# Moving x^T from TensorE to crossbar DMAs in an attention + gated-FFN kernel, with a later FFN and a re-planned order

## The chip, the cores and the metric

One core of one Trainium2 chip. The metric is the device time of one execution in microseconds (us), lower is better. Before: 307.08 us, median of 3 runs (306.74 to 307.47).

The names in what follows: PE is TensorE (matmuls and transposes), ACT is ScalarE, DVE is VectorE, and the sync engine (SP) issues DMAs. PSUM is the memory into which this kernel's matmuls and PE transposes write. A crossbar DMA is one that transposes what it moves (`dma_start_transpose`). It lands when its data is there. The granted clock is the share of its full speed at which PE was clocked.

## The reference, cut to what matters

Block-sparse attention over 4 batches, 8 heads, 768 positions and head size 64, followed by a gated FFN. The mask is 0 or 1 per block of 32 positions.

```python
scores = where(mask, q @ k.T / 8, -1e9)          # per batch and head, 768 x 768
attn = softmax(scores) @ v                       # -> x: (3072 tokens, 512)
gate = 1 / (1 + exp(-(x @ w_gate)))              # 512 -> 1536
out  = (gate * (x @ w_val)) @ w_out              # 1536 -> 512, float32
```

## The kernel before

The tokens are cut into 12 units of 256. A unit has four pairs of heads. For each pair the kernel makes the transposed scores (PE), exponentials (ACT), mask products (DVE), value products (PE), and the division by the row sum (DVE), which gives x16, tokens on partitions. The gate and value products of the FFN need x with features on partitions: x^T. The kernel before makes it with two PE transposes per pair and a copy out of PSUM by DVE or ACT:

```python
def turn(self, eng):
    for s in range(2):
        nc.tensor.transpose(
            m16(self.bank2.slot)[:, s * 128 : (s + 1) * 128], self.x16[:, s, :, :], ident)

def evac(self, eng):
    ...                                                   # allocates xT of the unit once
    copy(eng, xTs[self.n][0][:, self.p, :], m16(self.bank2.slot)[:, 0:UQ])

def xt(self):
    c = plan.add([(PE, 0.12)], self.turn, [self.normed], take=[self.bank2])
    ...
    plan.add([(DVE, 0.29), (ACT, 0.37)], self.evac, [c] + deps, free=[self.bank2])
```

All work is first entered as tasks in a `Plan`. The plan simulates a greedy schedule with rough costs, and then emits the instructions in the order that came out. Its costs never reach the chip; they only decide the order on each engine. At run time an engine takes its instructions in that order and waits on semaphores.

A unit's pass has six slots. A slot has two score steps, and one FFN part of an earlier unit to keep PE busy beside the exponentials:

```python
for sl in range(6):
    scores(flat[2 * sl : 2 * sl + 2])
    if sl >= 2:
        for i in range(3):
            ffn[n - 1].f(3 * (sl - 2) + i)       # gate and value products: 8 matmuls each
            if i == 0 and sl % 3 != 1:
                do(valued, do_value)             # value products of a pair
    elif n > 1:
        ffn[n - 2].y(sl)                         # output product: 12 matmuls
    ...
```

The softmax here doesn't subtract the row's maximum and nothing guards it: scores larger than these inputs give would overflow.

## Time and profile before

| | before |
|---|---|
| median | 307.08 us |
| span of the profiled run | 304.5 us |
| PE busy | 291.4 us |
| DVE / ACT busy | 200.9 / 210.7 us |
| one unit, in the steady part | 23.09 us |

First come the span, the busy times and the busy shares in 40 slices of the page of the kernel before (9 is 90% or more).

```profile
span 304.5 us, 7858 instructions
...
PE 291.4 (96%) x3326; PEld 209.6 (69%) x3326; DVE 200.9 (66%) x474; ACT 210.7 (69%) x340; POOL 48.5 (16%) x65
...
PE   3978999999999999999999999999999999999994
...
ACT  3669986776776776776776776776776776774431
PEclk9999999999999999999999999999999999999998
```

PE is full from the fifth slice (about 30 us) to the last but one. ACT is full only around the fourth and fifth slice.

A busy PE is not yet a PE with no time to give, since matmul ends are modelled. So the chain that ended last was read, in order of time, for one unit of the kernel before. Columns: start us, duration us, what. L571 is the output product, L466 the x transposes, L406 scores, L445 value products, L532 gate and value products.

```profile
94.91 2.59 PE m L571 x12
97.50 0.11 PE m L466 x2
97.61 0.54 PE s L406 x8
98.16 2.70 PE m L571 x12
100.85 0.11 PE m L466 x2
100.97 0.54 PE s L406 x8
...
109.05 0.11 PE m L466 x2
109.16 0.54 PE s L406 x8
...
118.01 2.59 PE m L571 x12
```

Each piece starts where the last one ended: PE's instruction stream alone sets the pace, 118.01 - 94.91 = 23.1 us per unit. A pair of transposes advances the chain by 0.11 us. The same transposes look far dearer in the table of groups of the kernel before (columns: busy us, mean ns of one, idle time ahead):

```profile
L466 PE MATMUL m<-ident,x 128*128 128x128 f16 x96 | 13.3, 221 | 0.1
L227 DVE COPY xT<-m 128x256 f16<-128x256 f16 x31 | 9.0, 292 | 10.9 <-PE m L466 10.9
L225 ACT COPY xT<-m 128x256 f16<-128x256 f16 x17 | 6.3, 371 | 0.0
```

221 ns is the time of one transpose through the pipeline. The next matmul starts long before that is over.

Last, the DMAs of the sync queue in the kernel before, with median us from issue to landing:

```profile
out_dram<-ysb SPq DMA_DIRECT2D x24, 256.0 KB, 2.0
kT<-kp SPq DMA_TRANSPOSE x3, 7.2
qT<-qp SPq DMA_TRANSPOSE x3, 7.1
```

The transposes of k and q, three of each and 768 KB apiece, are the only crossbar DMAs of this kernel.

### The profile page before, as it was taken

The page shows a single profiled execution, that of the slowest core. Times are in us where ns is not written, and L with a number is a line of the kernel's source. Part 1 is how long each engine was busy: PE and PEld are TensorE (multiplying, and loading weights), DVE is VectorE, ACT ScalarE, POOL GpSimd, SP SyncE. Part 2 cuts the span into 40 slices and gives each one's busy share as a digit, 9 for nine tenths or more (in the row PEclk, how much of TensorE's full clock was granted, in tenths as well). Part 3 has the DMA queues.
Part 4 walks back from the last instruction along what each step waited for, and adds up shares of the span by engine and source line. Part 5 has one row for each costly group of instructions (what it writes and reads, how often), then busy time and mean ns, then how long its engine had stood idle before and what let it go on. Part 6 is the DMA issues. An engine that isn't in the chain of part 4 may idle for free.

```text
span 304.5 us, 7858 instructions
## 1 busy us (share of the span) xinstructions
PE 291.4 (96%) x3326; PEld 209.6 (69%) x3326; DVE 200.9 (66%) x474; ACT 210.7 (69%) x340; POOL 48.5 (16%) x65
## 2 busy tenths in 40 slices
PE   3978999999999999999999999999999999999994
PEld 1355785786786786786686686687687687687771
DVE  4669878876676678676676577576576577576240
ACT  3669986776776776776776776776776776774431
POOL 8943000494000059200000000000000000000000
PEclk9999999999999999999999999999999999999998
DMA  7999999999500699930100580100100100100101
GB/s 100 181 203 202 206 204 183 223 160 131 128 1 2 158 154 124 154 74 2 71 2 0 113 168 1 71 2 2 69 2 2 69 2 4 69 2 2 69 2 70
DMA packets 62768, 25.75 MB, mean 85 GB/s; under 512 B 45812, under 2 KB 59660, under 8 KB 62732
## 3 DMA queue, kind: packets, MB, share of 16 engines
q0 software_dynamic: 40400, 14.16, 40.8%
q1 hardware_dynamic: 22332, 11.09, 15.0%
q8 instruction: 26, 0.43, 0.6%
q14 instruction: 10, 0.08, 0.1%
HBM read 28.39 MB, written 6.29 MB: 114 GB/s over the span
## 4 chain that ended last, share of the span: by engine, by line
PE 93%; ACT 2%; DMA 1%; DVE 1%; issue 1%; POOL 1%; POOLq 0%
PE m L532 42%; PE m L571 21%; PE s L406 13%; PE m L445 13%; PE m L466 2%; DMA v<-in_v_dram 1%; ACT pt L416 1%; PE m L303 1%; PE m L338 1%; ACT mask L225 1%; DVE pt L422 0%; DVE kT L227 0%; POOL k L178 0%; POOL q L178 0%; ACT ysb L582 0%
## 5 line engine op out<-in xcount | busy, mean ns | idle before, releaser
L416 ACT ACTIVATE pt<-s 128x1024 f16<-128x1024 f32 x144 | 140.1, 1026 | 4.6 <-PE s L406 3.7
L422 DVE TENSOR_TENSOR pt<-pt,mask 128x1024 f16<-128x1024 f16 x144 | 97.2, 687 | 38.8 <-ACT pt L416 38.4
L532 PE MATMUL m<-xT,wg 128*128 128x256 f16 x576 | 86.7, 273 | 0.0
L532 PE MATMUL m<-xT,wv 128*128 128x256 f16 x576 | 86.4, 273 | 0.0
L543 ACT ACTIVATE th<-m 128x256 f32<-128x256 f32 x144 | 54.6, 390 | 43.8 <-PE m L532 36.0
L548 DVE SCALAR_TENSOR_TENSOR ht<-th,m 128x256 f16<-128x256 f32 x144 | 57.3, 418 | 16.4 <-ACT th L543 14.8
L571 PE MATMUL m<-wo,ht 128*128 128x512 f16 x288 | 66.0, 379 | 0.0
L532 PEld LDWEIGHTS <-wv 128*128 128x128 f16 x576 | 56.3, 98 | 6.5
L532 PEld LDWEIGHTS <-wg 128*128 128x128 f16 x576 | 51.3, 97 | 12.5 <-issue 7.2
L445 PE MATMUL m<-vex,pt 128*128 128x65 f16 x1152 | 46.5, 196 | 1.8 <-ACT mask L225 1.6
L445 PEld LDWEIGHTS <-pt 128*128 128x128 f16 x1152 | 42.6, 99 | 7.6 <-issue 5.3
L571 PEld LDWEIGHTS <-ht 128*128 128x128 f16 x288 | 26.6, 98 | 30.7 <-issue 2.1
L406 PE MATMUL s<-qT,kT 64*128 64x256 f16 x576 | 47.1, 279 | 0.6 <-DVE qT L227 0.3
L582 ACT ACTIVATE ysb<-m 128x512 f32<-128x512 f32 x24 | 14.3, 597 | 35.3 <-PE m L571 35.3
L406 PEld LDWEIGHTS <-kT 64*128 64x128 f16 x576 | 22.0, 95 | 15.8 <-issue 8.6
L622 POOL DMA_DIRECT2D kp<-in_k_dram x16 | 13.0, 822 | 64.1 <-DMA kT<-kp 37.9
L455 DVE RECIPROCAL rz<-m 128x4 f32<-128x4 f32 x48 | 8.7, 182 | 19.5 <-PE m L445 18.8
L457 DVE TENSOR_TENSOR x<-m,rz 128x256 f16<-128x256 f32 x48 | 20.4, 425 | 1.7
L227 DVE COPY xT<-m 128x256 f16<-128x256 f16 x31 | 9.0, 292 | 10.9 <-PE m L466 10.9
L466 PE MATMUL m<-ident,x 128*128 128x128 f16 x96 | 13.3, 221 | 0.1
L622 POOL DMA_DIRECT2D qp<-in_q_dram x16 | 13.1, 827 | 0.7 <-DVE pt L422 0.4
L466 PEld LDWEIGHTS <-x 128*128 128x128 f16 x96 | 9.0, 98 | 6.1 <-DVE x L457 0.7
(36 smaller groups left out, 71.9 us busy)
## 6 DMA issues: line engine op xcount, KB each, us to landing
out_dram<-ysb SPq DMA_DIRECT2D x24, 256.0 KB, 2.0
v<-in_v_dram POOLq DMA_DIRECT2D x3, 768.0 KB, 10.9
wg<-in_moe_w_gate_dram POOLq DMA_DIRECT2D x4, 384.0 KB, 12.7
wv<-in_moe_w_val_dram POOLq DMA_DIRECT2D x4, 384.0 KB, 13.6
wo<-in_moe_w_out_dram POOLq DMA_DIRECT2D x3, 512.0 KB, 16.7
kp<-in_k_dram POOLq DMA_DIRECT2D x16, 96.0 KB, 5.1
qp<-in_q_dram POOLq DMA_DIRECT2D x16, 96.0 KB, 4.5
k<-in_k_dram POOLq DMA_DIRECT2D x4, 192.0 KB, 5.6
```

Of the source, the lines that this page charges most:

```text
L406: nc.tensor.matmul(score[self.bank.slot][:, a, i, :], kT[b % 2][o : o + D, p, t * 128 : (t + 1) * 128], qT[b % 2][o : o + D, p, u * UQ : ( ...
L416: nc.scalar.activation(self.pt, score[self.bank.slot], AF.Exp, bias=0.0, scale=SCALE)
L422: nc.vector.tensor_tensor(self.pt, self.pt, m.unsqueeze(1).broadcast_to([128, 2, 2, UQ]), op=ALU.mult,)
L445: nc.tensor.matmul(self.acc[:, s, a, :], self.steps[t // 2].pt[:, a, t % 2, s * 128 : (s + 1) * 128], vex[self.b % 2][:, 2 * self.p + a, t ...
L457: nc.vector.tensor_tensor(self.x16, self.acc[:, :, :, 0:D], rz.broadcast_to([128, 2, 2, D]), op=ALU.mult,)
L466: nc.tensor.transpose(m16(self.bank2.slot)[:, s * 128 : (s + 1) * 128], self.x16[:, s, :, :], ident,)
L532: nc.tensor.matmul(pg[:, i, :], w[:, c, f * 128 : (f + 1) * 128], xTs[self.n][0][:, c, :], start=(c == 0), stop=(c == 3),)
L543: nc.scalar.activation(th, spare[bank.slot][:, 0:UQ], AF.Tanh, bias=0.0, scale=0.5)
L548: nc.vector.scalar_tensor_tensor(self.ht[:, f, :], in0=box[0], scalar=1.0, in1=spare[bank.slot][:, UQ : 2 * UQ], op0=ALU.add, op1=ALU.mult,)
L571: nc.tensor.matmul(spare[bank.slot], self.ht[:, f, s * 128 : (s + 1) * 128], wo[:, f, :], start=(f == 0), stop=(f == NF - 1),)
L582: nc.scalar.activation(ysb, spare[bank.slot], AF.Copy, bias=0.0, scale=0.5)
L622: nc.gpsimd.dma_start(dst[:, p, :, a, :], src[b, 2 * p + a].rearrange("(n t) d -> n t d", t=NT),)
```

## The change

From unit 2 on, x^T of a pair comes from one crossbar DMA of 64 KB in place of two PE transposes and a copy. Such a DMA takes longer than the PE path. So the FFN parts come one slot later, and the plan counts a latency of 6 us for it. The output product is planned in three parts of four matmuls. The ring of x16 grows from 4 to 6 buffers.

```diff
+FFN_LAG = 3
+        def xbar(self, eng):
+            ...
+            nc.sync.dma_start_transpose(
+                xTs[self.n][0][:, self.p, :].rearrange("a (s n) -> a s n", s=2),
+                self.x16.rearrange("a s h d -> a (s h d)"),
+            )
         def xt(self):
+            if self.n >= 2:
+                deps = [used["xT"][self.n - XB]] if self.n >= XB else []
+                c = plan.add([(DMA, 0.05)], self.xbar, [self.normed] + deps, lag=6.0)
+                used["x16"].append(c)
+                xdone[self.n].append(c)
+                return
 ...
-            a = plan.add([(PE, 2.6)], mm, self.gated, at=land["wo", 2], take=[bank])
+            a = None
+            for f0 in range(0, NF, 4):
+                a = plan.add([(PE, 0.88)], y_mm(f0, f0 + 4),
+                    self.gated[f0 : f0 + 4] + ([] if a is None else [a]), ...)
 ...
-            if sl >= 2:
-                for i in range(3):
-                    ffn[n - 1].f(3 * (sl - 2) + i)
-                    ...
-            elif n > 1:
-                ffn[n - 2].y(sl)
+            part = parts.popleft() if n > 1 or sl >= FFN_LAG else []
+            for i, fn in enumerate(part):
+                fn()
+                if i == 0 and sl % 3 != 1:
+                    do(valued, do_value)
```

More of the change, by code (lines that the diff above doesn't have):

```diff
@@ L455, in norm @@
             nc.vector.reciprocal(rz, self.acc[:, :, :, D : D + 1])
-            self.x16 = work.tile([128, 2, 2, D], f16, tag="x16", bufs=4, name="x16")
+            self.x16 = work.tile([128, 2, 2, D], f16, tag="x16", bufs=6, name="x16")
             nc.vector.tensor_tensor(
@@ L483, in value @@
             read["pv", self.b, self.p] = [a]
-            self.normed = plan.add([(DVE, 0.6)], self.norm, [a] + ring("x16", 4),
+            self.normed = plan.add([(DVE, 0.6)], self.norm, [a] + ring("x16", 6),
                                    free=[self.bank])
-        def xt(self):
+        def xbar(self, eng):
+            if not xTs[self.n]:
+                xTs[self.n].append(
+                    work.tile([128, NP, UQ], f16, tag="xT", bufs=XB, name="xT")
+                )
+            nc.sync.dma_start_transpose(
+                xTs[self.n][0][:, self.p, :].rearrange("a (s n) -> a s n", s=2),
+                self.x16.rearrange("a s h d -> a (s h d)"),
+            )
+        def xt(self):
+            if self.n >= 2:
[4 more added lines that the diff above has]
+                return
             c = plan.add([(PE, 0.12)], self.turn, [self.normed], take=[self.bank2])
@@ L567, in y, with y_mm, go @@
             bank = Bank("m")
-            def mm(eng):
-                for f in range(NF):
-                    nc.tensor.matmul(
-                        spare[bank.slot],
-                        self.ht[:, f, s * 128 : (s + 1) * 128],
-                        wo[:, f, :],
-                        start=(f == 0),
-                        stop=(f == NF - 1),
-                    )
+            def y_mm(f0, f1):
+                def go(eng):
+                    for f in range(f0, f1):
+                        nc.tensor.matmul(
+                            spare[bank.slot],
+                            self.ht[:, f, s * 128 : (s + 1) * 128],
+                            wo[:, f, :],
+                            start=(f == 0),
+                            stop=(f == NF - 1),
+                        )
+                return go
             def evac(eng):
@@ L594, in evac @@
                 )
-            a = plan.add([(PE, 2.6)], mm, self.gated, at=land["wo", 2], take=[bank])
+            a = None
+            for f0 in range(0, NF, 4):
+                a = plan.add(
+                    [(PE, 0.88)],
+                    y_mm(f0, f0 + 4),
+                    self.gated[f0 : f0 + 4] + ([] if a is None else [a]),
+                    at=land["wo", f0 // 4],
+                    take=[bank] if f0 == 0 else [],
+                    lag=0.0 if f0 < 8 else None,
+                )
             if s == 1:
@@ L704 @@
     later(1)
+    parts = deque()
+    for F in ffn:
+        for i in range(4):
+            parts.append([lambda F=F, f=f: F.f(f) for f in range(3 * i, 3 * i + 3)])
+        parts.extend([[lambda F=F, s=s: F.y(s)] for s in range(2)])
     for n in range(1, len(units)):
@@ L718 @@
                 scores(run)
-            if sl >= 2:
-                for i in range(3):
-                    ffn[n - 1].f(3 * (sl - 2) + i)
-                    if i == 0 and sl % 3 != 1:
-                        do(valued, do_value)
-            elif n > 1:
-                ffn[n - 2].y(sl)
-            if sl == 0:
+            part = parts.popleft() if n > 1 or sl >= FFN_LAG else []
[3 more added lines that the diff above has]
+                    do(valued, do_value)
+            if not part and sl % 3 != 1:
                 do(valued, do_value)
@@ L736 @@
     do(valued, do_value)
-    ffn[-2].y(0)
-    do(turned, Pair.xt)
-    ffn[-2].y(1)
-    for f in range(NF):
-        ffn[-1].f(f)
-    ffn[-1].y(0)
-    ffn[-1].y(1)
+    for part in parts:
+        for fn in part:
+            fn()
+        do(turned, Pair.xt)
     plan.run()
```

## The prediction

> **What bounds the kernel.** TensorE. The page's first part has PE busy 291.4 of 304.5 us (96%); the stretch table shows 12.00 of 12.00 us from 36 us on. The chain of waits that ended last is 93% PE: gate/value products 42%, output product 21%, scores 13%, values 13%, x transposes 2%. ACT (210.7 us) and DVE (200.9 us) have slack. Idle PE time lies before 36 us and in the last 4 us. From unit 2 on a unit takes 23.1 us (output products start at 71.82, 94.91, 118.01 us in the chain).
>
> **Removed.** 80 of the 96 x transposes on PE, and 40 of the 48 evacuations to x^T (DVE 292 ns, ACT 371 ns each); the instruction lists agree. A transpose's duration is 221 ns, but it is pipelined: in the chain a pair takes 0.11 us, and the score group after it 0.54 us with or without a pair ahead. So 40 x 0.11 = 4.4 us of PE time, all on the critical path. The Trainium skill ("TensorE: Matmul & The Clock Gate", Part 4: PE-mode transpose) gives about 275 ns for one in a kernel; charging that would promise about 20 us, which this trace contradicts. The evacuations (about 12 us of DVE and ACT) are off the path, worth nothing directly.
>
> **Added.** 40 crossbar DMAs of 64 KB on the sync queue. The 768 KB ones of k and q (24 blocks of 128x128) take 3.5 to 6.2 us to issue and 7.2 us to land. Scaled to two blocks, I estimate 0.3 to 0.5 us of issue and 2.5 to 3.5 us to landing (the output DMA lands in 2.0). All stay on the one sync stream, as the Trainium skill ("DMA: Bandwidth & Descriptors", Silent corruption) requires.
>
> **Moved.** FFN parts come one slot (3.8 us) later. In the new order, between a unit's last value product and its first gate product stand 16 gate/value matmuls, three score groups, two output products and a value product: 1.75 + 3 x 0.54 + 2 x 2.70 + 0.77 = 9.5 us. Less 0.7 us of normalisation, 8 to 9 us hide a DMA of 3 us, even one slowed by the loads between 57 and 135 us. In the tail 7.8 us of products stand there. The big k/q transposes are queued after a unit's last small one and delay none that is urgent.
>
> Splitting the output product changes no PE work; it matters to the planner alone. Switches after a score group cost 0.11 us; they stay six per unit. Unit period: 23.09 - 0.44 = 22.65 us.
>
> In unit 1, the shift takes gate work away where ACT is full (11.87 of 12 us between 24 and 36 us); I allow 0 to 1.5 us of new idle PE time.
>
> **Prediction.** 307.08 - 4.4 + 0.6 = 303.3 us, range 301.8 to 306.2. Faster by over 2%: 0.04; within 2%: 0.90; slower by over 2%: 0.06.
>
> **Right if** the unit period is 22.65 us; 16 PE transposes are left; small crossbar DMAs land in 2.5 to 4 us, with no PE wait on them; DVE is near 190 us, ACT near 206 us; the first output product starts within 1.5 us of 48.8 us. **Wrong if** PE waits for x^T, the unit period stays at 23.1 us, or PE idles between 28 and 50 us.
>
> **What would make it wrong.** A small crossbar DMA taking over 8 us (fixed cost, the ordered sync queue blocked by an output DMA's wait, or contention with loads): some us in each of ten units, hence slower. Or neighbours' weight loads running better without the transposes: 1 to 2 us more gained.

## The result, and the profile after

| | before | after |
|---|---|---|
| median (4 runs each) | 306.91 us | 301.74 us (301.47 to 302.64) |
| span of the profiled run | 304.5 us | 299.7 us |
| PE busy | 291.4 us | 287.0 us |
| DVE / ACT busy | 200.9 / 210.7 us | 194.4 / 207.4 us |
| one unit, in the steady part | 23.09 us | 22.65 us |

The ratio after to before is 0.9836 (95% interval 0.9808 to 0.9863), hence faster by some 1.6%, within the band of 2%.

The page of the kernel after:

```profile
span 299.7 us, 7758 instructions
...
PE 287.0 (96%) x3246; PEld 203.1 (68%) x3246; DVE 194.4 (65%) x447; ACT 207.4 (69%) x327; POOL 48.5 (16%) x65
```

The chain of the kernel after for one unit. L589 is now the output product, L407 scores, L446 value products, L549 gate and value products:

```profile
94.96 2.69 PE m L589 x12
97.66 0.54 PE s L407 x8
98.20 2.70 PE m L589 x12
100.90 0.77 PE m L446 x24
101.67 0.54 PE s L407 x8
102.21 0.98 PE m L549 x8
...
117.61 1.40 PE m L589 x6
```

The pieces still follow one another without a gap, only the transposes are gone. The unit takes 117.61 - 94.96 = 22.65 us.

The transposes that are left, in the groups of the kernel after, and the crossbar DMAs among its DMA issues:

```profile
L467 PE MATMUL m<-ident,x 128*128 128x128 f16 x16 | 2.4, 231 | 0.1
```

```profile
xT<-x SPq DMA_TRANSPOSE x40, 2.4
```

The new DMAs land after 2.3 us at least, 2.4 in the median and 8.3 at most, among those of the 40 for which the trace has a landing. The last pair's DMA issued at 138.7 us, beside the loads of a later batch, took 5.1 us; the one issued at 161.3 us, with no loads, 2.3 us.

How much latency the order can hide is read from the timeline of the kernel after, around the last pair of a unit:

```profile
92.93 0.43 DVE L458 TENSOR_TENSOR x<-m,rz 128x256 f16<-128x256 f32 x1
93.38 1.17 SPq L493 DMA_TRANSPOSE xT<-x  x1
...
102.14 0.61 PE L549 MATMUL m<-xT,wg 128*128 128x256 f16 x4
```

The division ends at 93.36 us, the DMA is issued at once, and the first gate product that needs it starts 8.76 us later. With 2.4 us to landing, 6.4 us are spare. The 1.17 us in the second line is only the sync engine's issue. The Trainium skill ("Perfetto Trace Analysis", DMA Instruction — HWDGE) says that the profiler's window of such an instruction leaves out the data movement; this trace agrees, 1.17 us against 2.4 us to landing.

One measure is free of the jitter of the start: from the first gate product of the kernel to the end of the last output matmul. In the kernel before it goes from 31.37 to 300.08 us, 268.71 us; after, from 30.99 to 295.78 us, 264.79 us. This stretch is 3.92 us shorter. It is used below as "the stretch".

### The profile page after: what moved, and what is told of

Same layout as the page of the kernel before. It is cut to its first block, busy times and chain, and to the rows that moved or that the text cites. A ratio compares the mean times of both kernels' runs of the same rounds, so it can differ in the third digit from the quotient of the medians.

```text
span 299.7 us, 7758 instructions
## 1 busy us (share of the span) xinstructions
PE 287.0 (96%) x3246; PEld 203.1 (68%) x3246; DVE 194.4 (65%) x447; ACT 207.4 (69%) x327; POOL 48.5 (16%) x65
## 4 chain that ended last, share of the span: by engine, by line
PE 92%; ACT 2%; DMA 2%; DVE 2%; issue 1%; POOL 1%; POOLq 0%
PE m L549 43%; PE m L589 21%; PE s L407 13%; PE m L446 12%; DMA v<-in_v_dram 2%; ACT pt L417 1%; PE m L304 1%; PE m L339 1%; ACT mask L226 1%; DVE pt L423 0%; DVE kp L365 0%; POOL k L179 0%; PE m L467 0%; POOL q L179 0%; ACT xT L226 0%
## 5 line engine op out<-in xcount | busy, mean ns | idle before, releaser
L423 DVE TENSOR_TENSOR pt<-pt,mask 128x1024 f16<-128x1024 f16 x144 | 98.9, 689 | 50.2 <-ACT pt L417 49.8
L549 PE MATMUL m<-xT,wg 128*128 128x256 f16 x576 | 86.8, 273 | 0.0
L549 PE MATMUL m<-xT,wv 128*128 128x256 f16 x576 | 86.4, 273 | 0.0
L565 DVE SCALAR_TENSOR_TENSOR ht<-th,m 128x256 f16<-128x256 f32 x144 | 56.5, 417 | 20.8 <-ACT th L560 20.5
L589 PE MATMUL m<-wo,ht 128*128 128x512 f16 x288 | 65.9, 380 | 0.1
L549 PEld LDWEIGHTS <-wv 128*128 128x128 f16 x576 | 56.4, 98 | 6.5
L549 PEld LDWEIGHTS <-wg 128*128 128x128 f16 x576 | 50.4, 98 | 14.3 <-issue 9.3
L589 PEld LDWEIGHTS <-ht 128*128 128x128 f16 x288 | 26.6, 98 | 33.1 <-issue 4.2
L446 PEld LDWEIGHTS <-pt 128*128 128x128 f16 x1152 | 44.2, 99 | 6.2 <-issue 2.8
L446 PE MATMUL m<-vex,pt 128*128 128x65 f16 x1152 | 46.3, 196 | 1.8 <-ACT mask L226 1.6
L407 PE MATMUL s<-qT,kT 64*128 64x256 f16 x576 | 47.2, 278 | 0.6 <-DVE qT L228 0.3
L407 PEld LDWEIGHTS <-kT 64*128 64x128 f16 x576 | 21.8, 95 | 19.9 <-issue 16.0
L339 PE MATMUL m<-ident,pr 128*128 128x128 f16 x48 | 5.6, 264 | 0.4 <-DVE pr L330 0.4
L385 DVE COPY vex<-v 128x768 f16<-128x768 f16 x16 | 5.0, 361 | 1.4 <-DMA v<-in_v_dram 1.4
L179 POOL DMA_DIRECT2D v<-in_v_dram x7 | 5.5, 788 | 1.1 <-DMA wv<-in_moe_w_val_dram 1.1
```

What stands on the lines that cost most here:

```text
L407: nc.tensor.matmul(score[self.bank.slot][:, a, i, :], kT[b % 2][o : o + D, p, t * 128 : (t + 1) * 128], qT[b % 2][o : o + D, p, u * UQ : ( ...
L423: nc.vector.tensor_tensor(self.pt, self.pt, m.unsqueeze(1).broadcast_to([128, 2, 2, UQ]), op=ALU.mult,)
L446: nc.tensor.matmul(self.acc[:, s, a, :], self.steps[t // 2].pt[:, a, t % 2, s * 128 : (s + 1) * 128], vex[self.b % 2][:, 2 * self.p + a, t ...
L549: nc.tensor.matmul(pg[:, i, :], w[:, c, f * 128 : (f + 1) * 128], xTs[self.n][0][:, c, :], start=(c == 0), stop=(c == 3),)
L565: nc.vector.scalar_tensor_tensor(self.ht[:, f, :], in0=box[0], scalar=1.0, in1=spare[bank.slot][:, UQ : 2 * UQ], op0=ALU.add, op1=ALU.mult,)
L589: nc.tensor.matmul(spare[bank.slot], self.ht[:, f, s * 128 : (s + 1) * 128], wo[:, f, :], start=(f == 0), stop=(f == NF - 1),)
```

## The experiments

Theory A: the gain is the PE time of 80 transposes, 0.11 us a pair, and the order hides the DMA. Rival B: the new order is better by itself. Rival C: the relief of DVE and ACT gives the gain.

### The changed kernel once more

No edit; it is the yardstick of the other runs.

> The changed kernel, unaltered, as the yardstick of this call. Every theory: 5.0 to 5.3 us faster than before (ratio 0.983 to 0.984), unit period 22.65 us.

Measured: 301.59 us (301.29 to 302.45), before 306.29 us, ratio 0.9853 (0.9837 to 0.987). Stretch 264.78 us, as in the first profile. The gain is a little below what was expected, 4.5 to 4.7 us here.

### The new order without the DMAs

```diff
-            if self.n >= 2:
+            if self.n >= 99:
```

> The changed kernel with x^T made by PE transposes in every unit again: the later FFN parts, the split output product and the larger buffer ring stay, only the crossbar DMAs go. Theory A (the gain is the PE time of the 80 transposes): back to the time of before within 1 us, unit period 23.09 us, 96 PE transposes. Rival B (the new order itself is better): within 1 us of the changed kernel, 302 to 303 us.

Measured: 306.96 us (305.85 to 308.09), ratio to before 1.0021 (0.9999 to 1.0043). These two pieces of its chain, the first gate product and the last output products, bound its stretch:

```profile
31.91 1.85 PE m L549 x16
296.05 5.20 PE m L589 x24
```

The stretch is 269.34 us, 0.63 us longer than before, and a unit takes 23.09 us again (output products start at 96.66 and 119.75 us). Rival B falls: the order alone gains nothing. In unit 1 it seems to cost something, but the interval just includes none.

### Idle transposes beside the DMAs

```diff
+                t = plan.add([(PE, 0.12)], self.turn, [self.normed], take=[self.bank2],
+                             free=[self.bank2])
-                c = plan.add([(DMA, 0.05)], self.xbar, [self.normed] + deps, lag=6.0)
+                c = plan.add([(DMA, 0.05)], self.xbar, [self.normed, t] + deps, lag=6.0)
```

> The changed kernel plus the 80 PE transposes done for nothing: their results stay in PSUM, nothing copies them out, x^T still comes by DMA. Theory A (PE time): 4 to 5 us slower than the changed kernel, about 306.5 us, though DVE and ACT keep their relief (DVE near 194 us). Rival C (the relief of DVE and ACT, or PSUM banks, gives the gain): within 1 us of the changed kernel.

Measured: 313.33 us (312.53 to 313.88), ratio 1.023 (1.0211 to 1.0249): 11.7 us slower than the changed kernel, far more than either theory said. The chain of this run in a steady unit shows why (L467 are the idle transposes, L446 value products, L551 gate and value products):

```profile
222.61 0.54 PE s L407 x8
223.16 0.89 PE m L446 x24
224.05 0.02 issue
224.07 0.19 DVE rz L456
224.27 0.02 issue
224.29 0.44 DVE x L458
224.72 0.05 issue
224.77 0.28 PE m L467 x2
225.06 2.62 PE m L551 x24
```

The new tasks made the planner change the order. It put a transpose straight behind the value product that feeds it, so PE stands still while DVE divides. These waits come to 5.3 us, and PE is busy 6.4 us longer than in the yardstick (293.0 against 286.6 us); together that is the 11.7 us. The experiment changed two things.

### The same with the evacuations

```diff
+                plan.add([(DVE, 0.29), (ACT, 0.37)], self.evac_idle, [t], free=[self.bank2])
```

> The same plus the 40 evacuations by DVE or ACT into a scratch tile, so all of the old work beside the DMAs. Theory A: no slower than the idle transposes alone, within 0.7 us. Rival C: most of the 5 us are lost only in this run.

Measured: 313.02 us (311.59 to 313.64), ratio 1.0212 (1.0188 to 1.0236). No slower than the idle transposes alone, though DVE and ACT have their 40 copies again (DVE 200.4, ACT 214.6 us busy). Against rival C, with the reservation that both runs share the disturbed order.

### Idle transposes that the planner does not see

```diff
         def mm(eng):                      # of a score group
+            if late and late[0][1] < 0:
+                x, _ = late.popleft()     # an x16 of at least one group ago
+                for s in range(2):
+                    nc.tensor.transpose(<score bank>[:, s * 128 : (s + 1) * 128], x[:, s, :, :], ident)
             for pr, st in run:
                 st.qk()                   # overwrites that bank
+            for e in late:
+                e[1] -= 1
```

> The idle transposes again, since the first run of them let the planner change the order of everything else. Now the planner never sees them: each pair is put in front of a score group that comes at least one group after its normalisation, into the score bank that the group overwrites. The order of all other PE instructions is that of the changed kernel. Theory A (0.11 us of PE time a pair, some 38 pairs): 4 to 5 us slower than the changed kernel, about 306 us, unit period 23.09 us, no wait of PE for the normalisation. If the 11.7 us of the first run were the transposes' own cost: about 313 us again.

Measured: 305.68 us (304.69 to 306.51), 4.1 us slower than the changed kernel, ratio to before 0.9977 (0.9956 to 0.9999). The chain of this run, L522 being the idle transposes:

```profile
188.09 2.70 PE m L603 x12
190.79 0.11 PE s L522 x2
190.90 0.54 PE s L407 x8
191.44 2.70 PE m L603 x12
```

37 pairs were run. The stretch is 268.91 us, 4.13 us longer than the yardstick's: 4.13 / 37 = 0.11 us a pair. The next unit's output product starts at 211.18 us, a unit of 23.09 us. Here nothing but PE work came back, and with it nearly the whole gain went. DVE and ACT kept their relief (195.2 and 208.7 us busy), and so did the PSUM bank that the old transposes took, since these use a score bank. That shows theory A.

### DVE gets its work back, PE does not

```diff
+            if self.n >= 2:               # after the division
+                xd = work.tile([128, 2, 2, D], f16, tag="xd", bufs=2, name="xd")
+                nc.vector.tensor_copy(xd, self.acc[:, :, :, 0:D])
```

> The changed kernel plus one idle copy by DVE per pair from PSUM to a scratch tile (40 copies, about 0.3 to 0.4 us each), so that DVE has its evacuation work back while PE has not. Theory A: within 0.6 us of the changed kernel, DVE busy 207 to 211 us. Rival C (relief of DVE gives the gain): 3 to 5 us slower.

Measured: 301.94 us (301.14 to 303.66), stretch 264.77 us, DVE busy 206.3 us (slightly under what I expected). 12 us more of DVE work cost nothing. Rival C falls as to DVE; as to ACT it falls by the run before, in which ACT kept its relief and the gain went all the same.

### The output product in one piece

```diff
-            for f0 in range(0, NF, 4):
+            for f0 in range(0, NF, NF):
-                    [(PE, 0.88)], y_mm(f0, f0 + 4), self.gated[f0 : f0 + 4] + ...
+                    [(PE, 2.6)], y_mm(0, NF), self.gated + ...
```

> The changed kernel with the output product planned in one piece again. PE has the same work in almost the same order, and each matmul waits for its own slice of ht as before. Every theory of mine: within 0.6 us of the changed kernel. If starting the output product before all gates are done is worth something: 1 us or more slower.

Measured: 301.81 us (301.29 to 302.27), stretch 264.91 us. The split is worth nothing in this order.

### FFN parts in their old slots

```diff
-FFN_LAG = 3
+FFN_LAG = 2
```

> The changed kernel with FFN_LAG 2, so the parts keep the slots of before. Theory A with the DMA's latency hidden by the order: the planner, which counts 6 us for a DMA, puts the gate products in larger groups, but PE has the same work less transposes; within 1 us of the changed kernel (301 to 303 us). If the shift by a slot is what hides the DMA: PE waits for x^T in each unit, 305 us or more.

Measured: 319.96 us (319.37 to 321.94), ratio 1.0468 (1.0437 to 1.0499), 18 us slower than the changed kernel. I had expected 301 to 303 us for the case that the planner copes. PE waits for the DMA only once, for 5.0 us. The bulk is again the plan: counting 6 us per DMA, it held the gate products back and set two value products ahead of them with only scores between. So PE has nothing to do while ACT and DVE prepare the second one: in nine units it waits for ACT's exponentials (6.3 us in all), and in most of them then for DVE's mask products (1.9 us). A unit takes 23.97 us (from 196.98 to 220.95 us in the chain).

### Old slots, planned with 3.5 us

```diff
-FFN_LAG = 3
+FFN_LAG = 2
-                c = plan.add([(DMA, 0.05)], self.xbar, [self.normed] + deps, lag=6.0)
+                c = plan.add([(DMA, 0.05)], self.xbar, [self.normed] + deps, lag=3.5)
```

> FFN_LAG 2 as before, but planned with a DMA latency of 3.5 us in place of 6, which keeps the planner from setting two value products in a row ahead of the gate products. Between the issue of a unit's last x^T DMA and its first use there remain some 4 us. The 18 us of the first lag run were the planner's order, not the DMA's: now the unit period is 22.65 us where no loads run (DMA lands in 2.4 us), and PE waits for x^T some 2 to 4.5 us in each of the two units whose x^T falls beside the loads of the next batch; 304 to 309 us in all. If the shift by a slot is not needed at all: 301 to 302.5 us.

Measured: 320.16 us (318.3 to 321.98), ratio 1.0449 (1.0409 to 1.049). Half right: undisturbed units take 22.64 us (second output product at 101.80, the next at 124.44 us). The total is a miss by 11 us. PE waits for x^T three times, 14.1 us, and the longest wait is not mainly one for a slow DMA. This is the timeline of the sync engine in that run:

```profile
124.48 3.65 SPq L376 DMA_TRANSPOSE kT<-kp  x1
128.43 3.66 SPq L376 DMA_TRANSPOSE qT<-qp  x1
132.19 1.29 SPq L493 DMA_TRANSPOSE xT<-x  x1
```

And PE's first gate product in the timeline of PE, with the wait ahead of it:

```profile
137.77 0.37 PE L549 MATMUL m<-xT,wg 128*128 128x256 f16 x1 [8.89 <-DMA xT<-x]
```

The big transposes of k and q stand ahead of the urgent small one in the sync engine's order, and their issue alone takes 7.7 us. The division that feeds the small one ended at 124.58 us, so it was held back for 7.6 us; after that it took some 5.5 us itself. In the plan a crossbar DMA occupies the issuing engine for 0.01 or 0.05 us, so the plan does not see this. The third wait, some 2.1 us (14.1 less the other two) that ends at 209.46 us, follows the same pair in the next batch; the first, 3.13 us, falls beside loads. After the long waits the granted clock is down to 0.79 (82 to 90 us) and 0.76 (137 to 145 us), and PE's busy time is 2.8 us more than the changed kernel's. In the changed kernel the two big transposes come just after the last small one of a unit, with the same plan blindness; one slot more of slack and a lucky order keep it harmless.

### More latency, order untouched

The last pair of each unit goes through two plain SBUF copies before its crossbar DMA:

```diff
+            xs = self.x16
+            if self.p == NP - 1:
+                for i in range(2):
+                    xh = work.tile([128, 2, 2, D], f16, tag=f"xh{i}", bufs=1, name="xh")
+                    nc.sync.dma_start(xh, xs)
+                    xs = xh
```

> The changed kernel, order untouched, but the last pair of each unit goes through two plain SBUF copies by DMA before its crossbar DMA, some 4 us more latency. In the trace 8.8 us lie between the issue of that pair's DMA and the first gate product that needs it, and it lands after 2.4 us. Theory A with 6.4 us of slack: same as the changed kernel within 0.6 us. If latency is barely hidden: 20 us and more slower.

Measured: 310.64 us (308.39 to 312.61), ratio 1.0141 (1.0101 to 1.0181). A miss as to the sum, right as to the quiet units. PE waits for x^T in just two of ten units, both beside loads of a later batch:

```profile
82.11 0.27 PE L555 MATMUL m<-xT,wg 128*128 128x256 f16 x1 [1.63 <-DMA xT<-xh]
153.69 0.27 PE L555 MATMUL m<-xT,wg 128*128 128x256 f16 x1 [3.48 <-DMA xT<-xh]
```

A copy lands in 1.8 us in quiet units, but in 4.0 to 5.2 us there. I had taken the quiet figure for all ten units. The second wait has an after-cost, seen in the stretches of this run (the length of the stretch, PE busy, then the other engines, the granted clock and the DMAs):

```profile
153.00:156.00 3.00, 2.31 (x33) 2.07 (x33) 0.49 (x2) 0.38 (x1) 0.00 (x0) 0.78 0.60 204
156.00:160.00 4.00, 4.00 (x32) 2.83 (x30) 1.93 (x6) 1.77 (x4) 0.00 (x0) 0.74 0.10 17
160.00:164.00 4.00, 4.00 (x58) 3.32 (x56) 3.12 (x6) 3.56 (x7) 0.00 (x0) 1.00 0.00 0
```

PE is busy in the second line, but at 0.74 of its clock. The Trainium skill ("TensorE: Matmul & The Clock Gate", Why this matters for your kernels) advises no PE idle gaps over about 3 us between bursts; the 3.48 us here agree. The 1.63 us wait shown above left the clock at 1.00 (82 to 86 us). The limit is not a sharp one, though: in the run with four copies, told next, a wait of 2.16 us is followed by a clock of 0.58 (310 to 314 us), and one of 2.07 us by 1.00 (264 to 268 us). Waits of 5.1 us and 2.1 us more PE busy time make 7.2 of the 7.5 us that this profile is longer than the yardstick's.

With four copies in place of two:

> The same with four copies, some 8 us more latency, 10.5 us in all against 8.8 us. Theory A: PE now waits for x^T about 1.5 to 2.5 us in each of ten units, 15 to 25 us slower than the changed kernel, and the trace names the DMA as the releaser. If the slack is larger than I read: no change.

Measured: 334.37 us (333.19 to 336.18), ratio 1.0929 (1.089 to 1.0968), 33 us slower than the changed kernel. Ten waits, 25.3 us together: 0.3 to 0.9 us in most quiet units of the middle, 1.3 to 2.2 us in the last four, 6.5 and 9.5 us beside the loads. Four copies add less than I had taken in quiet units (4 x 1.8 us), and more beside loads. The direction is theory A's: once the latency passes 8.8 us, PE waits, and the trace names the DMA.

### One unit further

```diff
-            if self.n >= 2:
+            if self.n >= 1:
```

> A step further: the crossbar DMA for unit 1 too, which removes four more pairs of PE transposes. Theory A: 0.4 us faster than the changed kernel (0.2 to 0.8), if these DMAs, which run beside the weight loads, still land within 8 us. If they do not: PE waits near 57 us and the time is 0 to 3 us longer.

Measured: 300.73 us (300.43 to 301.16), ratio to before 0.9829 (0.9808 to 0.985), correct. The stretch is 264.20 us, 0.58 us shorter than the yardstick's for four pairs fewer: the 0.44 us of the transposes and a little more. (An idle 0.08 us of PE near 49 us, which the changed kernel has, is gone here too.) It is the fastest kernel here, ahead of both. The medians are of two calls and the ratios' intervals overlap, so the stretch is the better evidence for this small gain.

## Why the prediction was right, point by point

- **The bound and the gain.** Right. PE's instruction stream was the limit, and 0.11 us a pair was the right cost: the unit went from 23.09 to 22.65 us, exactly as predicted, and the idle transposes that the planner did not see gave 0.11 us a pair back. Neither the order alone, nor DVE's work, nor the split changed the time by more than 0.7 us.
- **The pipelined cost, not the duration.** Right. 80 x 221 ns would be 17.7 us; the change of the stretch is 3.9 us.
- **The sum.** 4.4 us less and 0.6 us more were predicted, 3.8 us net. The stretch shows just this: 269.34 - 264.79 = 4.55 us for the transposes and 268.71 to 269.34, 0.63 us, for the new order, 3.92 us net. That the 0.6 came out is luck: it stood for new idle PE time in unit 1, and what cost 0.63 us was mostly something else (see below). By wall time 5.2 us (medians of the first comparison) and 4.7 us (second) were gained, so the time is better than the point forecast by about 1 us: 0.9836 x 307.08 = 302.0 us, while the raw median of 301.74 us lies 0.06 us below the low end of the range. The term that was left out is at the ends. In the profiles the first gate product came 0.38 us earlier, which varies from run to run (30.28 to 31.91 us), and from the last output matmul to the end of the span it took 4.42 us before and 4.45 us in the order alone, but 3.65 to 4.0 us in six kernels with the small DMAs (after, its repeat, the unseen idle transposes, the DVE copies, the product in one piece, from unit 1). Of the other six kernels with them five lie at 3.7 to 4.0 us, but the one with four copies at 4.3 us. The wait for the last output DMA is 1.5 us in both kernels, so the half microsecond lies behind it. What causes it stays open.
- **New idle time in unit 1.** 0 to 1.5 us were allowed. Next to none came: PE is full from 36 to 49 us, and between 49 and 50 us it idles for 0.08 us, just ahead of the first output product. That product starts at 49.51 us, within the 1.5 us of 48.8 us that the prediction named. The 0.63 us of the order alone are mostly extra switches: after the first gate product its chain has six score groups of four matmuls, the kernel before has two. Four such groups in place of two of eight take 0.24 us more (0.33 against 0.54 us each), and the piece after each of the two added switches takes 0.11 us more (gate products 0.98 against 0.87 us). With the idle 0.08 us this makes 0.54 us. It is an estimate from the chains; no run tested it alone.
- **DMA latency.** 2.4 us measured, 2.5 to 3.5 expected. The issue was under-estimated: 1.17 us, not 0.3 to 0.5. Scaling the 24-block DMA down left out a fixed part. It cost nothing here because the sync engine has time. All 40 go out on the sync queue, and no run had transposes on two queues, so none tests the rule that the prediction cites for it.
- **The slack.** 9.5 us less 0.7 were predicted, 8.76 us measured. Right for quiet units. Beside loads the last pair's DMA took up to 5.1 us where the trace gives a figure, so the margin is smaller there, and the added-latency runs broke first in those units.
- **Busy times.** DVE 194.4 us (190 expected) and ACT 207.4 us (206): the planner gave the two engines another share of the copies.
- **What would make it wrong.** The named danger, the ordered sync queue and the loads, is real. Two experiments with one slot less ran into it at once. The changed kernel does not, though two of its small DMAs do take 8.3 us, more than the 8 us named. They were issued at 126.4 and 128.4 us, right after the two big ones and beside loads, and they are the first two of their unit; the gate products wait for the last one anyway. So what counts is the landing of a unit's last DMA, not of any.

## What to carry to other kernels

Where one engine's instruction stream is the chain, cost a removed instruction by how far it moves that chain, not by its duration: here 0.055 us against 0.22 us. Work can go to a slower path almost for free (the order that makes the room cost 0.63 us here) as long as the time between result and use covers the slow path's worst landing, which here came beside bulk loads and behind big issues on the same queue, not its median. When a planner decides the order, an experiment that adds a task also changes the order; compare the instruction lists, or add the work where the planner can't see it.

## What the Trainium skill lacked or had wrong

- "TensorE: Matmul & The Clock Gate", Part 4: PE-mode transpose, tells only durations, about 275 ns in a kernel. Here the duration is 219 to 231 ns in the groups, and the cost to a full PE stream is 4.13 us for 74 transposes, 0.056 us each. Part 4 does not give the second number, which is the one that a saving is worked out from. Part 2 of the page has spacings only for plain matmuls 128 columns wide, about 56 ns alone and about 81 ns in a stream with weight loads; it does not say which holds for transposes.
- "DMA: Bandwidth & Descriptors", Issuing engines are not separate DMA queues, calls the issue time "usually small relative to the DMA itself". For the crossbar DMAs here it is about half to three quarters: 1.17 us of 2.4 us for 64 KB, and 3.5 to 6.2 us of 5.7 to 8.2 us for 768 KB. Two big ones ahead of a small one held it back for 7.6 us, and PE then waited 8.9 us. I found no page that warns of an urgent DMA standing behind a long issue.
- No page gives landing times of small crossbar or SBUF-to-SBUF DMAs with and without bulk loads beside them: 2.3 us quiet and up to 8.3 us for 64 KB through the crossbar, 1.8 us quiet and 4.0 to 5.2 us for a plain copy of the same size. "VectorE: DVE Perf Modes", The three transpose paths, has one figure, 1309 ns for a 128x128 block through the crossbar, without saying up to what point or beside what.
